# Moving the shift filter to channel-major tiles and the layer-norm scaling to ScalarE in a convolution and feed-forward kernel

## The chip, the cores and the metric

The kernel runs on one core of a Trainium2 chip. A time is the device time of one execution in microseconds (us). Kernels were timed in rounds together with the kernel before on the same chip. One core has five instruction streams that matter here, each working through its own list in order: TensorE (PE, matrix multiplication), VectorE (DVE, elementwise), ScalarE (ACT, elementwise with functions, here also the reader of most of PE's results), GpSimd (POOL) and SyncE (SP, which here only starts DMA transfers). The order inside each stream is settled when the kernel is built.

## The reference, cut to what matters

```python
def _layernorm(x): ...                       # (x - mean) / sqrt(var + 1e-5), no weights
# S = 2048 rows, D = 640 channels, F = 1728
k_shift[s] = sum_t k[s - t] * shift_k[:, t]  # 4 taps: the shift filter
kv = k_shift * v
y  = causal_convolution(kv, ssm_k)           # 2048 taps per channel, by FFT in the reference
y  = y + kv * ssm_D
h  = x + layernorm(x) * y                    # x is A_q
h2 = h + (silu(layernorm(h) @ w_gate) * (layernorm(h) @ w_up)) @ w_down
```

All tensors are bfloat16. One remark on correctness: at these input sizes the convolution branch is so small beside `x` that the plain comparison with the reference can't see an error in it. The kernels whose values matter here were therefore also compared in values with `k`, `v` and `shift_k` enlarged 16 times and `ssm_k` 512 times; all had a relative error of 0.0085.

## The kernel before: the parts that matter

The sequence is cut into four blocks of 512 rows. The convolution is done block by block with a 1024-point spectral transform as matmuls: `X[j]` is the spectrum of block j of `kv`, `H[p]` the spectra of the long filter, and `pair(j, p)` adds a complex product of 128x2560 tiles to `A[j + p]` on VectorE. Since the transform uses even and odd parts about the block's middle, a `fold` adds and subtracts the mirrored half first.

The shift filter has rows on partitions. Four shifted copies of each row are loaded, multiplied by weights spread over all partitions (`w4`), added and multiplied by `v`; the mirrored half comes from a TensorE matmul with a reversal matrix and a ScalarE copy:

```python
    def front_half(t, v):                                  # VectorE, 128x1280 each
        ks = [t[:, :, s, :] for s in range(4)]
        for s in (3, 2, 1, 0):
            nc.vector.tensor_mul(ks[s], ks[s], w4[:, 3 - s:4 - s, :].to_broadcast([P, 2, D]))
        nc.vector.tensor_add(ks[3], ks[3], ks[2])          # ... two more adds, then * v
    def fold(ta, tb):
        kv, kvr = tb[:, :, 3, :], ta[:, :, 2, :]
        nc.vector.tensor_add(xe, kv, kvr)
        nc.vector.tensor_sub(xo, kv, kvr)
```

The layer norm takes sums on ScalarE (`stats`), the power -1/2 on POOL and the scaling on VectorE. The scaled rows go through a DMA transpose to become the moving side of the feed-forward's first matmuls (the weights are the stationary side):

```python
    def ln_rstd(mv, n, tag):
        # ... va = variance + eps, two small VectorE operations
        nc.gpsimd.tensor_tensor(rs[:], va[:], mhalf[:, 0:n, :], op=ALU.pow)
    def ln_apply(out_, in_, mv, rs):
        nc.vector.tensor_scalar(out_, in_, mv, rs, op0=ALU.subtract, op1=ALU.mult)
    def to_ffn(m, mv, rs, x, hT):
        # ... for each of two row groups:
            ln_apply(hl[:], x[:, q, :], mv[:, s, 0:1], rs[:, s, :])
            nc.sync.dma_start_transpose(hT[:, :, q * P:(q + 1) * P], hl[:])
```

In the feed-forward each of 14 chunks takes ten 128x512 matmuls into a PSUM tile `pf`, of which there are two. ScalarE must read both halves of it (an eviction) before TensorE may use that buffer again:

```python
                nc.scalar.activation(sg[:z, :], pg[:z, :], ACT.Silu)
                nc.scalar.copy(uc[:z, :], pu[:z, :])
                nc.vector.tensor_mul(tT[:z, c * MB:(c + 1) * MB], sg[:z, :], uc[:z, :])
```

The main loop interleaves the convolution of block j + 1 with the feed-forward of block j by priorities.

## Time and profile before

The median is 327.9 us (327.0 to 329.5, four runs). Milestones from the TensorE timeline, in us from the span's start:

| | feed-forward 0 up / down starts | 1 | 2 | 3 | last matmul |
|---|---|---|---|---|---|
| before | 80.0 / 124.5 | 141.1 / 180.2 | 213.6 / 252.2 | 274.9 / 307.0 | 323.1 |

First the page's busy line of the kernel before: for each engine its busy us, the share of the span and the instructions. Over the whole span TensorE is the busiest.

```profile
PE 280.5 (86%) x1580; PEld 153.7 (47%) x1580; DVE 239.2 (73%) x334; ACT 171.4 (52%) x334; POOL 37.6 (11%) x33
```

An average over stages with different limits hides the bound. The next view is the table of stretches of the kernel before. Its columns are the stretch, its length, the busy us (and instructions) of each engine, the granted TensorE clock, the DMA share and the GB/s.

```profile
77.30:257.60 180.30, 162.59 (x886) 84.32 (x883) 172.36 (x224) 100.67 (x199) 22.43 (x11) 0.97 0.51 145
257.60:274.90 17.30, 14.41 (x101) 9.22 (x102) 11.37 (x25) 7.33 (x17) 3.51 (x4) 1.00 0.30 72
274.90:327.20 52.30, 48.23 (x252) 24.33 (x252) 9.24 (x18) 15.01 (x28) 2.00 (x2) 0.96 0.27 74
```

In the middle stretch, up to the end of the last spectral product, VectorE idles only 180.3 - 172.4 = 7.9 us. After it comes a tail of 69.6 us, which holds 14.41 + 48.23 = 62.6 us of TensorE work. The chain that ended last agrees that VectorE paces most of it (shares of the span by engine):

```profile
DVE 49%; PE 29%; DMA 6%; ACT 6%; issue 5%; POOL 4%; SPq 0%; DVEq 0%; POOLq 0%; ACTq 0%
```

The timeline of the kernel before, VectorE's last product and TensorE's longest gaps of the middle and end. Columns are start, length, engine, line, operation, output and inputs with count, and in brackets the idle time just before and what ended it.

```profile
204.81 0.72 PE L131 MATMUL ps<-xln,IJ 128*128 128x320 bf16 x4 [2.92 <-DVE hl L280]
212.05 1.25 PE L131 MATMUL ps<-k,IJ 128*128 128x320 bf16 x4 [6.52 <-DVE k L178]
...
256.12 1.49 DVE L251 TENSOR_TENSOR A_1383<-A_1383,T 128x2560 bf16<-128x2560 bf16 x1
...
274.89 1.39 PE L370 MATMUL pf<-hT,wg 128*128 128x512 bf16 x3 [2.82 <-DMA hT<-hl]
```

Two lines of the groups of instructions show what the change takes from VectorE: the filter's multiplications, and one of the groups of scalings (columns: line, engine, operation, names, shapes, count, then busy us and mean ns of one, then idle before).

```profile
L170 DVE TENSOR_TENSOR k<-k,w_91 128x1280 bf16<-128x1280 bf16 x24 | 19.1, 818 | 4.9 <-DMA k<-in_A_k_dram 4.9
...
L280 DVE TENSOR_SCALAR xln<-x,mv_826,rs_842 128x640 bf16<-128x640 bf16 x4 | 1.7, 444 | 0.9 <-POOL rs_842 L276 0.9
```

### The profile page before, as it was taken

Reading aid. Unit: us, or ns where it says so; the run is one execution under the profiler, and the core shown is the slowest. Engines: PE = TensorE matmul, PEld = TensorE weight load, DVE = VectorE, ACT = ScalarE, POOL = GpSimd, SP = SyncE. Lnnn points to the kernel's source line nnn. Section 1 sums busy time; section 2 is a strip of 40 time slices with the busy share of each in tenths; the row PEclk is TensorE's granted clock in tenths of the full one; section 3 lists DMA queues with packets and bytes.
Section 4 is the critical chain, followed back from the end, with each engine's and each line's share of the span. In section 5 each row is a group of like instructions: output and inputs, shape, how many; then the busy total and the mean of one; then the engine's idle time right before and its main releaser. Section 6 shows DMA issues by size and latency. Waiting matters only on the chain.

```text
span 327.2 us, 4271 instructions
## 1 busy us (share of the span) xinstructions
PE 280.5 (86%) x1580; PEld 153.7 (47%) x1580; DVE 239.2 (73%) x334; ACT 171.4 (52%) x334; POOL 37.6 (11%) x33
## 2 busy tenths in 40 slices
PE   2396888689699899989999896199999996999995
PEld 0254466456354356644445564034454662444563
DVE  0693398965999899899998999999969972122122
ACT  3138784897875438039748206964475080544300
POOL 6000001010000302510001071200010120000020
PEclk9999599999999999999999999679999998999999
DMA  7999900059687424536686503525525114355011
GB/s 231 373 311 224 331 0 3 21 119 376 198 296 211 116 79 124 101 98 166 167 216 227 173 20 95 123 73 144 155 58 141 41 40 100 99 151 132 2 40 41
DMA packets 67440, 45.94 MB, mean 140 GB/s; under 512 B 25614, under 2 KB 64846, under 8 KB 67420
## 3 DMA queue, kind: packets, MB, share of 16 engines
q1 hardware_dynamic: 66876, 44.29, 48.2%
q0 software_dynamic: 544, 1.39, 1.2%
q8 instruction: 12, 0.20, 0.2%
q14 instruction: 8, 0.07, 0.1%
HBM read 38.46 MB, written 2.62 MB: 126 GB/s over the span
## 4 chain that ended last, share of the span: by engine, by line
DVE 49%; PE 29%; DMA 6%; ACT 6%; issue 5%; POOL 4%; SPq 0%; DVEq 0%; POOLq 0%; ACTq 0%
PE pf L390 8%; PE pf L370 7%; PE pf L372 6%; DVE tT L379 4%; PE pf L214 4%; DVE k L170 3%; DVE T L250 3%; DMA hT<-hl 3%; DVE T L243 3%; PE ps L224 3%; DVE y L322 2%; DVE o L395 2%; DVE T L241 2%; DMA A_101<-in_A_k_dram 2%; DMA k<-in_A_k_dram 2%
## 5 line engine op out<-in xcount | busy, mean ns | idle before, releaser
L370 PE MATMUL pf<-hT,wg 128*128 128x512 bf16 (+1 forms) x280 | 72.2, 388 | 5.2 <-DMA hT<-hl 3.1
L372 PE MATMUL pf<-hT,wu 128*128 128x512 bf16 (+1 forms) x280 | 72.4, 385 | 0.0
L390 PE MATMUL pf<-wd,tT 128*128 128x320 bf16 x448 | 65.1, 299 | 0.0
L376 ACT ACTIVATE sg<-pf 128x512 bf16<-128x512 f32 (+1 forms) x56 | 33.4, 596 | 53.4 <-PE pf L372 52.4
L390 PEld LDWEIGHTS <-tT 128*128 128x128 bf16 x448 | 41.3, 97 | 23.1 <-issue 8.4
L379 DVE TENSOR_TENSOR tT<-sg,uc 128x512 bf16<-128x512 bf16 (+1 forms) x56 | 23.5, 419 | 32.0 <-ACT uc L378 31.9
L370 PEld LDWEIGHTS <-wg 128*128 128x128 bf16 (+1 forms) x280 | 27.4, 100 | 40.0 <-issue 7.5
L372 PEld LDWEIGHTS <-wu 128*128 128x128 bf16 (+1 forms) x280 | 28.1, 100 | 33.0 <-issue 2.8
L214 PE MATMUL pf<-wd,tT 128*128 128x320 bf16 x192 | 30.5, 317 | 8.7 <-POOL wd L448 3.8
L214 PEld LDWEIGHTS <-tT 128*128 128x128 bf16 x256 | 26.0, 102 | 21.7 <-issue 10.6
L378 ACT CAST uc<-pf 128x512 bf16<-128x512 f32 (+1 forms) x56 | 32.5, 581 | 0.0
L268 ACT ACTIVATE junk<-x 128x640 bf16<-128x640 bf16 x32 | 23.7, 741 | 9.5 <-DVE x L324 8.4
L400 POOL DMA_INDIRECT out_dram<-o,idx x8 | 15.7, 1968 | 88.2 <-DVE o L395 80.1
L269 ACT ACTIVATE junk<-x 128x640 bf16<-128x640 bf16 x32 | 23.7, 740 | 0.9
L170 DVE TENSOR_TENSOR k<-k,w_91 128x1280 bf16<-128x1280 bf16 x24 | 19.1, 818 | 4.9 <-DMA k<-in_A_k_dram 4.9
L395 DVE TENSOR_TENSOR o<-pf,x 128x640 bf16<-128x640 f32 x16 | 13.1, 818 | 12.1 <-PE pf L390 12.1
L224 PEld LDWEIGHTS <-WX 128*128 128x128 bf16 x128 | 13.2, 105 | 17.6 <-issue 7.1
L307 ACT COPY es<-ps 128x640 f32<-128x640 f32 x8 | 5.5, 693 | 27.7 <-PE ps L304 27.7
L224 PE MATMUL ps<-k,WX 128*128 128x320 bf16 x96 | 15.4, 298 | 2.4 <-DVE k L185 2.2
L322 DVE TENSOR_TENSOR y<-es,ps 128x640 bf16<-128x640 f32 x16 | 12.5, 813 | 0.7 <-PE ps L314 0.7
L132 ACT CAST x<-ps 128x640 bf16<-128x640 f32 x8 | 5.1, 691 | 14.8 <-DVE o L395 14.8
L216 ACT CAST G_95<-pf 128x640 bf16<-128x640 f32 x8 | 5.6, 696 | 13.7 <-PE pf L214 13.7
(175 smaller groups left out, 337.0 us busy)
## 6 DMA issues: line engine op xcount, KB each, us to landing
k<-in_A_k_dram SPq DMA_DIRECT2D x6, 1280.0 KB, 6.1
wg<-in_B_w_gate_dram SPq DMA_DIRECT2D x24, 320.0 KB, 3.2
wu<-in_B_w_up_dram SPq DMA_DIRECT2D x24, 320.0 KB, 3.8
wd<-in_B_w_down_dram SPq DMA_DIRECT2D x1, 2080.0 KB
v<-in_A_v_dram SPq DMA_DIRECT2D x5, 320.0 KB, 3.4
A_102<-in_A_k_dram SPq DMA_DIRECT2D x1, 1280.0 KB, 11.3
x<-in_A_q_dram SPq DMA_DIRECT2D x4, 320.0 KB, 5.3
xln<-in_A_q_dram SPq DMA_DIRECT2D x4, 320.0 KB, 3.2
```

The costliest lines, as they stand in the source:

```text
L170: nc.vector.tensor_mul(ks[s], ks[s], w4[:, 3 - s:4 - s, :].to_broadcast([P, 2, D]))
L214: nc.tensor.matmul(ps[:, h, 0:NH], WG[:, kt, ct * P:(ct + 1) * P], gT[p][:, kt, h * NH:(h + 1) * NH], start=(kt == 0), stop=(kt == 3))
L224: nc.tensor.matmul(ps[:, h, 0:NH], WX[:, kt, ct * P:(ct + 1) * P], src[:, kt, h * NH:(h + 1) * NH], start=(kt == 0), stop=(kt == 1))
L268: nc.scalar.activation(junk[:], src, ACT.Copy, scale=1.0 / D, accum_out=mv[:, 0:1])
L269: nc.scalar.activation(junk[:], src, ACT.Square, scale=D ** -0.5, accum_out=mv[:, 1:2])
L370: nc.tensor.matmul(pg[:z, :], wg[:, kt, cc * P:cc * P + z], hT[:, kt, :], start=(kt == 0), stop=(kt == 4))
L372: nc.tensor.matmul(pu[:z, :], wu[:, kt, cc * P:cc * P + z], hT[:, kt, :], start=(kt == 0), stop=(kt == 4))
L376: nc.scalar.activation(sg[:z, :], pg[:z, :], ACT.Silu)
L378: nc.scalar.copy(uc[:z, :], pu[:z, :])
L379: nc.vector.tensor_mul(tT[:z, c * MB:(c + 1) * MB], sg[:z, :], uc[:z, :])
L390: nc.tensor.matmul(ps[:, h, 0:NH], tT[:z, c * MB + m * P:c * MB + (m + 1) * P], wd[:z, c, h * NH:(h + 1) * NH], start=(c == 0), stop=(c == ...
L395: nc.vector.tensor_add(r3(o[:]), ps[:, :, 0:NH], r3(x[:, m, :]))
```

## The change

The intent: take work off VectorE, the bound of the middle stretch, and give it to ScalarE, which is half idle, and to DMA. For blocks 1 to 3, (1) `k` and `v` are loaded by DMA transposes, so that channels lie on partitions and a tap is a multiplication by one number per partition; (2) taps 1 and 3 run on ScalarE; (3) the mirror is a reversed operand of the fold; (4) the folded tile goes back to rows on partitions by five DMA transposes; (5) both layer-norm scalings run on ScalarE, which needs the shift -mean/std as an extra small POOL operation; (6) a block's filter and `pair(0, 3)` are issued earlier than before. Block 1's filter, on the other hand, is held back until the last sums and scalings of block 0 are in the list (`issue_after`). The diff's core:

```diff
+    def front_cm(kT, vT, xeo):
+        def tap(dst, s):
+            for c in range(5):
+                src = kT[:, c, 16 - s:16 - s + MB]
+                w = wT[:, c, s:s + 1]
+                if s in (1, 3):
+                    nc.scalar.activation(dst[:, c, :], src, ACT.Copy, scale=w)
+                else:
+                    nc.vector.tensor_scalar(dst[:, c, :], src, w, None, op0=ALU.mult)
         ... taps, three adds and the product with vT: 128x2560 each
+        lo, hi = p1[:, :, 255::-1], p1[:, :, 256:512]
+        nc.vector.tensor_add(vT[:, :, 0:256], hi, lo)
+        nc.vector.tensor_sub(vT[:, :, 256:512], hi, lo)
+        for c in range(5):
+            nc.sync.dma_start_transpose(xeo[:, :, c * P:(c + 1) * P], vT[:, c, :])
     ...
+    def ln_shift(mv, rs, n, tag):
+        nc.gpsimd.tensor_tensor(nm[:], mv[:, :, 0:1], rs[:], op=ALU.mult)
+    def ln_apply_act(out_, in_, nm, rs):
+        nc.scalar.activation(out_, in_, ACT.Identity, bias=nm, scale=rs)
     ... x_norm and to_ffn of blocks 1 to 3 call these two
     ... in the main loop:
-                xeo[n] = conv_front(n, z - 5000, z)
-            if n == 2:
-                A[3] = sp("A1")
-                pair(0, 3)
+                xeo[n] = conv_front(n, z - 9500, z - 7500)
     ...
             if n == 1:
                 A[2] = sp("G1")
                 pair(0, 2)
+                A[3] = sp("A1")
+                pair(0, 3)
+                prio(z + 3500)
                 pair(1, 1)
```

More of the change, by code (lines that the diff above doesn't have):

```diff
@@ L145 @@
     WI = cpool.tile([P, 8, 256], BF16, name="WI")
-    w4 = cpool.tile([P, 4, D], BF16, name="w4")
+    wT = cpool.tile([P, 5, 4], FP32, name="wT")
+    wTb = cpool.tile([P, 5, 4], BF16, name="wTb")
     Drow = cpool.tile([1, D], BF16, name="Drow")
@@ L155 @@
     T = spec.tile([P, 4, D], BF16, name="T")
+    w4 = T
     H, X, A = [G[0], None, G[2], G[3]], {}, {}
@@ L187, in fold, with load_front @@
         return xe, xo
-    def load_front(j, half):
-        t = front.tile([P, 2, 4, D], BF16, name="k", bufs=2)
-        load_k(nc.sync, t[:], j, half)
-        v = front.tile([P, 2, D], BF16, name="v")
-        load2(nc.sync, v[:], vv, j, half)
-        return t, v
-    def conv_front(j, p_load, p_calc):
-        ts = []
-        for half in (0, 1):
-            prio(p_load + 20 * half)
-            t, v = load_front(j, half)
-            prio(p_calc + 50 * half)
-            for _ in front_half(t, v[:]):
-                pass
-            if half == 0:
-                mirror(t[:, :, 3, :], t[:, :, 2, :])
-            ts.append(t)
-        return fold(*ts)
+    def load_front(j):
+        kT = front.tile([P, 5, MB + 16], BF16, name="kT")
+        nc.sync.dma_start_transpose(kT[:], kk[j * MB - 16:(j + 1) * MB, :])
+        vT = front.tile([P, 5, MB], BF16, name="vT")
+        nc.sync.dma_start_transpose(vT[:], vv[j * MB:(j + 1) * MB, :])
+        return kT, vT
@@ new lines, in front_cm @@
+    def front_cm(kT, vT, xeo):
[7 more added lines that the diff above has]
+                    nc.vector.tensor_scalar(dst[:, c, :], src, w, None, op0=ALU.mult)
+        pt = lambda: front.tile([P, 5, MB], BF16, name="pt", bufs=2)
+        p3, p2 = pt(), pt()
+        tap(p3, 3)
+        tap(p2, 2)
+        yield
+        nc.vector.tensor_add(p2[:], p2[:], p3[:])
+        yield
+        p1 = pt()
+        tap(p1, 1)
+        p0 = kT[:, :, 16:16 + MB]
+        tap(p0, 0)
+        yield
+        nc.vector.tensor_add(p1[:], p1[:], p0)
+        yield
+        nc.vector.tensor_add(p1[:], p1[:], p2[:])
+        yield
+        nc.vector.tensor_mul(p1[:], p1[:], vT[:])
+        yield
+        lo, hi = p1[:, :, 255::-1], p1[:, :, 256:512]
+        nc.vector.tensor_add(vT[:, :, 0:256], hi, lo)
+        yield
+        nc.vector.tensor_sub(vT[:, :, 256:512], hi, lo)
+        for c in range(5):
+            nc.sync.dma_start_transpose(xeo[:, :, c * P:(c + 1) * P], vT[:, c, :])
+        yield
@@ L209, in g_transform, with new_xeo @@
+    def new_xeo():
+        return front.tile([P, 4, D], BF16, name="xeo")
+    def conv_front(j, p_load, p_calc):
+        prio(p_load)
+        kT, vT = load_front(j)
+        prio(p_calc)
+        xeo = new_xeo()
+        for _ in front_cm(kT, vT, xeo):
+            pass
+        return xeo[:, 0:2, :], xeo[:, 2:4, :]
     def g_transform(p, cts=range(NCT)):
@@ L267, in stats @@
         junk = front.tile([P, D], BF16, name="junk")
-        nc.scalar.activation(junk[:], src, ACT.Copy, scale=1.0 / D, accum_out=mv[:, 0:1])
-        nc.scalar.activation(junk[:], src, ACT.Square, scale=D ** -0.5, accum_out=mv[:, 1:2])
+        nc.scalar.activation(junk[:], src, ACT.Copy, scale=-1.0 / D, accum_out=mv[:, 0:1])
+        return nc.scalar.activation(junk[:], src, ACT.Square, scale=D ** -0.5, accum_out=mv[:, 1:2])
     def ln_rstd(mv, n, tag):
@@ L279, in ln_apply @@
     def ln_apply(out_, in_, mv, rs):
-        nc.vector.tensor_scalar(out_, in_, mv, rs, op0=ALU.subtract, op1=ALU.mult)
+        return nc.vector.tensor_scalar(out_, in_, mv, rs, op0=ALU.add, op1=ALU.mult)
+    def ln_shift(mv, rs, n, tag):
+        nm = small.tile([P, n, 1], FP32, name="nm" + tag)
+        nc.gpsimd.tensor_tensor(nm[:], mv[:, :, 0:1], rs[:], op=ALU.mult)
+        return nm
+    def ln_apply_act(out_, in_, nm, rs):
+        nc.scalar.activation(out_, in_, ACT.Identity, bias=nm, scale=rs)
     def load_x(j, eng):
@@ L295, in x_norm @@
                 stats(x[:, q, :], mv[:, q, :])
+            rs = ln_rstd(mv[:], 4, "1")
+            nm = ln_shift(mv, rs, 4, "1")
+            for q in range(4):
+                ln_apply_act(xl[:, q, :], x[:, q, :], nm[:, q, :], rs[:, q, :])
+            return
         rs = ln_rstd(mv[:], 4, "1")
@@ L324, in add_row @@
         nc.vector.tensor_add(x[:, q, :], x[:, q, :], y[:])
-        stats(x[:, q, :], mv[:, s, :])
+        return stats(x[:, q, :], mv[:, s, :])
     def add_rows(m, es, po, x, xln):
@@ L332, in add_rows, with to_ffn @@
         return mv, ln_rstd(mv[:], 2, "2")
-    def to_ffn(m, mv, rs, x, hT):
+    def to_ffn(m, mv, rs, x, hT, on_act=True):
+        if on_act:
+            nm = ln_shift(mv, rs, 2, "2")
         for s in range(2):
@@ L337, in to_ffn @@
             hl = rot.tile([P, D], BF16, name="hl")
-            ln_apply(hl[:], x[:, q, :], mv[:, s, 0:1], rs[:, s, :])
+            if on_act:
+                ln_apply_act(hl[:], x[:, q, :], nm[:, s, :], rs[:, s, :])
+            else:
+                last = ln_apply(hl[:], x[:, q, :], mv[:, s, 0:1], rs[:, s, :])
             nc.sync.dma_start_transpose(hT[:, :, q * P:(q + 1) * P], hl[:])
+        return None if on_act else last
     def new_hT():
@@ L419 @@
     nc.gpsimd.dma_start(out=Drow[:], in_=A_ssm_D.partition_broadcast(1))
+    nc.gpsimd.dma_start(out=wTb[:], in_=A_shift_k.rearrange("(c p) j -> p c j", p=P))
+    nc.gpsimd.tensor_copy(wT[:], wTb[:])
     load2(nc.sync, v0[:, 0:2, :], vv, 0, 0)
@@ L470 @@
         po = inv_odd(A[0], 0)
-        t1, v1 = load_front(1, 0)
-        f1 = front_half(t1, v1[:])
+        k1, v1 = load_front(1)
         es1 = inv_even(A[0], 1)
-        drain(f1, 2)
         po1 = inv_odd(A[0], 1)
@@ L486 @@
         g_transform(2, range(3, 4))
-        add_row(1, 1, es1, po1, x0, xl0, mvb)
-        to_ffn(0, mva, rsa, x0, hT[0])
+        act0 = add_row(1, 1, es1, po1, x0, xl0, mvb)
+        to_ffn(0, mva, rsa, x0, hT[0], False)
         g_transform(2, range(4, 6))
-        drain(f1, 1)
         rsb = ln_rstd(mvb[:], 2, "2")
-        drain(f1, 1)
-        to_ffn(1, mvb, rsb, x0, hT[0])
+        dve0 = to_ffn(1, mvb, rsb, x0, hT[0], False)
         g_transform(2, range(6, 8))
-        t2 = front.tile([P, 2, 4, D], BF16, name="k", bufs=2)
-        load_k(nc.sync, t2[:], 1, 1)
-        v2 = sp("A1")[:, 0:2, :]
-        load2(nc.sync, v2, vv, 1, 1)
         wd = big.tile([P, NF, D], BF16, name="wd")
@@ L501 @@
         nc.sync.dma_start(out=wd[0:64, 13, :], in_=B_w_down[13 * P:FF, :])
-        g_transform(3, range(0, 4))
-        drain(f1)
-        mirror(t1[:, :, 3, :], t1[:, :, 2, :])
-        g_transform(3, range(4, 8))
+        g_transform(3)
     prio(3000)
-    drain(front_half(t2, v2))
-    xeo[1] = fold(t1, t2)
+    later = ExitStack()
+    later.enter_context(tc.issue_after(dve0.ins))
+    later.enter_context(tc.issue_after(act0.ins))
+    xeo1 = new_xeo()
+    drain(front_cm(k1, v1, xeo1))
+    xeo[1] = xeo1[:, 0:2, :], xeo1[:, 2:4, :]
     prio(3200)
@@ L535 @@
             x_norm(xin[n], xln[n])
+            later.close()
             hT[n] = inverse(A[n], xin[n], xln[n])
```

## The prediction

> **What bounds it now.** VectorE paces the middle: the stretch table shows DVE busy 172.4 of 180.3 us between 77.3 and 257.6 us, ScalarE 100.7; TensorE waits 11 us around 200 to 213 us. In the DVE timeline a 128x2560 bf16 product starts every 1.40 us, a 128x1280 one every 0.735. The Trainium skill, "VectorE: DVE Perf Modes", section "The perf-mode tier table", caps bf16 tensor_tensor at 2x and lets tensor_scalar reach 4x, which fits. After DVE's last spectral product (257.6 us) comes a tail of 69 us: inverse, layer norm, the end of feed-forward 2, feed-forward 3 (14 x 2.16 + 16.1 = 46.3 us, TensorE at its full pace).
>
> **What the change does.**
> - Filter on DVE, per block 1 to 3: was 18 x 0.735 = 13.2 us. Now 10 taps of 128x512 (estimate 0.27 us each, from 0.36 for 128x640 with two scalars), 4 x 1.40, 2 folds of 1280 with a reversed operand (0.735 if that keeps 2x, 1.4 if not): 9.8 to 11.1 us. Saves 2 to 3.4.
> - Layer-norm scaling of blocks 1 to 3 leaves DVE: 8 x 0.36 = 2.9 us per block. In all DVE saves about 16 us.
> - ScalarE gains 30 taps and 24 scalings, loses 6 mirror copies. The skill, "ScalarE: Activation LUTs", section "What ACT_TABLE_LOAD costs", adds about 93 ns per pointer operand; from the 0.64 us pace of the 128x640 passes I estimate 0.6 us a tap, 0.8 a scaling: busy 171 to about 205 us. Not a bound, but in order.
> - DMA: redundant row loads become transposes, and the folded result goes through five transposes per block (about 1.2 us of issue each, 2.6 to landing, read from those of hl): about 7 us between fold and transform that did not exist. Other pairs and the next filter fill it; for block 1 I expect 1 to 3 us of DVE idle.
> - The 4.9 us DVE wait for k at 72 us goes. In exchange hbuild and filter work that DVE did in gaps before 69 us now runs after block 0's norm, which should finish 1 to 2 us sooner.
>
> **Critical path.** Up to feed-forward 0's end (about 125 us before its down projection) I expect almost no gain. DVE then reaches its last spectral product at 236 to 240 us. The gain is not passed on whole: in the new order TensorE then still has 3.5 chunks of feed-forward 2 up, its down and feed-forward 3 to do, about 77 us instead of 69. That hides the last layer norm, so the wait of 2.8 us before feed-forward 3 goes. 238 + 77.4 + about 1.5 us gives 317.
>
> **Predicted: 317 us, 309 to 324 (8 in 10). Faster by over 2%: 0.75; within 2%: 0.22; slower: 0.03.**
>
> **What would show it.** DVE busy 239 to about 222 us; ACT about 205; taps near 0.35 us long, folds 0.82 (or 1.5); last spectral product at 236 to 240 us; no TensorE gap over 3 us between feed-forwards 2 and 3; the 11 us gap before feed-forward 2 shrunk to about 4; feed-forward 0's down projection starting where it did.
>
> **What would make it wrong.** Large transposes that land late or block the in-order SP queue, so weights come late; ScalarE stalling in order at a scaling that waits for POOL or an hl buffer, delaying the next SiLU; folds at 1x; or, the other way, TensorE ahead of DVE everywhere, when its own work (about 213 us after 79 us) would give 300.

## The result and the profile after

The change made the kernel slower: 338.8 us median (337.6 to 339.3, four runs) beside 327.9 us. The ratio is 1.032 (95% interval 1.027 to 1.037). A ratio here is the mean time of one kernel's fast runs over that of the other's in the same rounds, so it is not quite the ratio of the medians quoted.

| | feed-forward 0 up / down starts | 1 | 2 | 3 | last matmul |
|---|---|---|---|---|---|
| before | 80.0 / 124.5 | 141.1 / 180.2 | 213.6 / 252.2 | 274.9 / 307.0 | 323.1 |
| after | 76.6 / 123.5 | 143.9 / 199.8 | 221.6 / 270.2 | 286.6 / 317.0 | 333.2 |

The loss shows in two places: the up projection of feed-forward 1 took 55.9 us instead of 39.1, and that of feed-forward 2 took 48.6 us instead of 38.6. Not all of this is waiting: in the tables of stretches below each of the two holds 200 matmuls instead of 179 and 180, as a part of the next block's inverse moved into it (5.0 us of TensorE in each, beside 0 and 1.05 us before). What lies between gained: from down 1 to up 2 it is 21.8 us instead of 33.4, and from down 2 to up 3 it is 16.4 instead of 22.7. The page's busy line of the kernel after shows that the planned move did happen: VectorE lost 17.5 us and ScalarE gained 29.6.

```profile
PE 282.5 (84%) x1553; PEld 153.2 (45%) x1568; DVE 221.7 (66%) x304; ACT 201.0 (60%) x382; POOL 36.7 (11%) x44
```

The table of stretches of the kernel after, cut where feed-forward 0 starts, the last spectral product ends and feed-forward 3 starts. (The table of the kernel before starts 2.75 us ahead of its feed-forward 0, where VectorE's wait for `k` ends.)

```profile
76.60:253.80 177.20, 149.59 (x765) 75.32 (x774) 152.85 (x189) 119.74 (x231) 20.56 (x18) 0.95 0.46 114
253.80:286.60 32.80, 29.73 (x183) 17.10 (x182) 11.71 (x25) 15.08 (x32) 3.78 (x6) 1.00 0.35 92
286.60:336.90 50.30, 46.39 (x250) 23.91 (x252) 10.08 (x19) 15.02 (x28) 1.92 (x2) 1.00 0.28 79
```

Counted from the start of feed-forward 0 in both kernels (in the kernel before the stretch is then 177.55 us long, with VectorE busy 169.63), VectorE was busy 16.8 us less in the middle stretch, but the stretch shrank by only 0.4 us: VectorE's idle time went from 7.9 to 24.4 us. And more of TensorE's work was left for the tail: 29.73 + 46.39 = 76.1 us, 13.5 us more than before, so the tail grew from 69.6 to 83.1 us. The view of the chain that ended last doesn't help here. "Issue", time in which an engine waited for nothing that the profile shows, is now its largest part, and its longest pieces lie ahead of POOL instructions (33.3 us before the store at 130.18 us), where the view finds no releaser; it shows no cause:

```profile
issue 39%; PE 31%; ACT 12%; POOL 7%; DMA 5%; DVE 4%; SPq 2%; POOLq 0%; DVEq 0%; ACTq 0%
```

The waits view says more. First the one line of it from the kernel before (columns: engine, what waited, for what: us in total, times, longest us):

```profile
DVE tT L379 <- ACT uc L378: 31.9, 15, 7.1
```

Then the kernel after:

```profile
DVE tT L436 <- ACT uc L435: 56.1, 29, 8.2
...
PE pf L427 <- ACT uc L435: 11.0, 9, 2.6
...
PE ps L262 <- DMA xeo<-vT: 8.5, 5, 2.3
...
ACT hl L326 <- POOL nm_1579 L322: 7.8, 1, 7.8
```

VectorE waits for ScalarE's evictions, TensorE waits for the same evictions and for the new transposes, and ScalarE waits for POOL. The timeline around the start of feed-forward 1 shows these waits in place; which of them made the difference only the experiments can say. First POOL: a store of the block before stands ahead of the power of the norm; then comes the new shift.

```profile
130.18 1.15 POOL L457 DMA_INDIRECT out_dram<-o,idx  x1 [33.51 <-DVE va_894 L312]
131.37 0.97 POOL L314 TENSOR_TENSOR rs_897<-va_894,mhalf 128x2 f32<-128x2 f32 x1
132.41 0.20 POOL L322 TENSOR_TENSOR nm_899<-mv_879,rs_897 128x2 f32<-128x2 f32 x1
```

Then ScalarE, with its two pairs of scalings, the second of which waits 1.96 us more for POOL:

```profile
132.65 1.73 ACT L326 ACTIVATE hl<-x,nm_899,rs_897 128x640 bf16<-128x640 bf16 x2 [1.38 <-POOL nm_899 L322]
...
138.99 1.73 ACT L326 ACTIVATE hl<-x,nm_947,rs_945 128x640 bf16<-128x640 bf16 x2 [1.96 <-POOL nm_947 L322]
```

Then the queue of SyncE, where a line is a group of DMA issues with the time from the start of the first to the end of the last. The transposes of `hT` run to 142.46 us, and the five transposes to `xeo` stand behind them in the same queue. It looks as if the late scalings had pushed all this back; e1 below shows that they had not:

```profile
133.60 8.86 SPq L395 DMA_TRANSPOSE hT<-hl  x4
...
143.17 6.43 SPq L232 DMA_TRANSPOSE xeo<-vT  x5
```

And TensorE, which has the next block's transform in the middle of the up projection's list and so stops there:

```profile
143.86 0.58 PE L427 MATMUL pf<-hT,wg 128*128 128x512 bf16 x1 [3.57 <-DVE G_955 L289]
...
148.26 0.30 PE L262 MATMUL ps<-xeo,WX 128*128 128x320 bf16 x1 [0.98 <-DMA xeo<-vT]
150.78 2.02 PE L262 MATMUL ps<-xeo,WX 128*128 128x320 bf16 x7 [2.23 <-DMA xeo<-vT]
...
155.79 1.24 PE L427 MATMUL pf<-hT,wg 128*128 128x512 bf16 x5
...
167.38 2.24 PE L427 MATMUL pf<-hT,wg 128*128 128x512 bf16 x5 [2.40 <-ACT uc L435]
...
173.82 1.86 PE L427 MATMUL pf<-hT,wg 128*128 128x512 bf16 x5 [2.43 <-ACT uc L435]
```

While TensorE stands at `xeo`, no up projection comes out, so VectorE has its product of gate and up as the next instruction and nothing to put in (8.15 us of idle before 154.80 us). The 3.57 us before 143.86 us are put down to VectorE by the view, but the last transpose of `hT` lands at about that time too. The last two gaps are ScalarE's. Ahead of the first, its list held copies of the transform and sums of the norm until the eviction at 166.67 us; ahead of the second, before 173.21 us, it worked in order through the wait for POOL (2.12 us) and four scalings (3.35 us) that stand ahead of an eviction:

```profile
169.94 3.35 ACT L326 ACTIVATE xln<-x,nm_1484,rs_1482 128x640 bf16<-128x640 bf16 x4 [2.12 <-POOL nm_1484 L322]
173.21 0.56 ACT L435 CAST uc<-pf 128x512 bf16<-128x512 f32 x1
```

There is a second price of such gaps. In the list above five 128x512 matmuls take 1.24 us at 155.79 and 2.24 us after the gap at 167.38. The tables of stretches for the two up projections that lost show the granted clock (third number from the right). In the kernel before:

```profile
141.10:180.20 39.10, 36.78 (x179) 16.90 (x176) 37.90 (x52) 26.98 (x54) 1.04 (x1) 1.00 0.64 183
213.60:252.20 38.60, 38.11 (x180) 17.81 (x181) 35.45 (x45) 22.02 (x41) 1.57 (x1) 0.96 0.43 113
```

And in the kernel after. The clock is lower in the first, 0.88 instead of 1.00, but not in the second:

```profile
143.90:199.80 55.90, 46.59 (x200) 21.31 (x204) 44.46 (x56) 33.20 (x66) 2.70 (x2) 0.88 0.41 101
221.60:270.20 48.60, 40.57 (x200) 19.66 (x205) 35.45 (x47) 36.55 (x76) 2.72 (x5) 1.00 0.42 109
```

The Trainium skill, "TensorE: Matmul & The Clock Gate", section "Part 1: The HAM clock gate (the "warmup" mystery)", says that the array's clock is halved after an idle window and comes back after some microseconds of sustained work. This trace agrees in kind: the granted clock was 0.57 between 150 and 153 us and 0.64 between 168 and 172 us, both right after gaps. How much of the loss the clock made was not tested.

The same chain of POOL, scaling, transpose returns at the start of feed-forward 2, in POOL and ScalarE of the kernel after. Here the store took 3.57 us, and the power and the shift took longer as well:

```profile
210.34 3.57 POOL L457 DMA_INDIRECT out_dram<-o,idx  x1 [5.90 <-DVE va_1574 L312]
213.94 1.77 POOL L314 TENSOR_TENSOR rs_1577<-va_1574,mhalf 128x2 f32<-128x2 f32 x1
215.79 0.92 POOL L322 TENSOR_TENSOR nm_1579<-mv_1559,rs_1577 128x2 f32<-128x2 f32 x1
...
216.74 1.73 ACT L326 ACTIVATE hl<-x,nm_1579,rs_1577 128x640 bf16<-128x640 bf16 x2 [7.76 <-POOL nm_1579 L322]
```

All this is a reading of one trace, and it names at least four suspects: the scaling on ScalarE (with POOL's extra step), the taps on ScalarE, the five transposes to `xeo`, and the new order. The experiments separate them.

### The profile page after: what moved, and what is told of

The parts are those of the page before. It is cut to its first block, busy times and chain, and to the rows that moved or that the text cites. A ratio compares the mean times of both kernels' runs of the same rounds, so it can differ in the third digit from the quotient of the medians.

```text
span 336.9 us, 4280 instructions
## 1 busy us (share of the span) xinstructions
PE 282.5 (84%) x1553; PEld 153.2 (45%) x1568; DVE 221.7 (66%) x304; ACT 201.0 (60%) x382; POOL 36.7 (11%) x44
## 4 chain that ended last, share of the span: by engine, by line
issue 39%; PE 31%; ACT 12%; POOL 7%; DMA 5%; DVE 4%; SPq 2%; POOLq 0%; DVEq 0%; ACTq 0%
PE pf L447 8%; PE pf L429 7%; PE pf L427 7%; PE pf L252 5%; ACT junk L306 3%; ACT junk L307 2%; PE ps L262 2%; DMA A_102<-in_A_k_dram 2%; DMA out_dram<-o,idx 2%; POOL out_dram L457 1%; PE ps L365 1%; ACT A_2035 L264 1%; SPq L232 1%; DMA wu<-in_B_w_up_dram 1%; PE ps L355 1%
## 5 line engine op out<-in xcount | busy, mean ns | idle before, releaser
L429 PE MATMUL pf<-hT,wu 128*128 128x512 bf16 (+1 forms) x275 | 73.7, 393 | 0.2
L447 PE MATMUL pf<-wd,tT 128*128 128x320 bf16 (+1 forms) x448 | 64.7, 299 | 1.9 <-ACT uc L435 1.6
L447 PEld LDWEIGHTS <-tT 128*128 128x128 bf16 (+1 forms) x448 | 41.2, 97 | 25.6 <-issue 10.1
L252 PE MATMUL pf<-wd,tT 128*128 128x320 bf16 x192 | 29.6, 312 | 6.2 <-POOL wd L507 3.5
L252 PEld LDWEIGHTS <-tT 128*128 128x128 bf16 x256 | 25.7, 100 | 19.2 <-issue 8.5
L306 ACT ACTIVATE junk<-x 128x640 bf16<-128x640 bf16 x32 | 24.1, 754 | 4.0 <-DVE x L375 3.8
L262 PE MATMUL ps<-xeo,WX 128*128 128x320 bf16 x96 | 17.7, 321 | 9.3 <-DMA xeo<-vT 8.5
L262 PEld LDWEIGHTS <-WX 128*128 128x128 bf16 x128 | 13.5, 108 | 26.0 <-issue 12.5
L307 ACT ACTIVATE junk<-x 128x640 bf16<-128x640 bf16 x32 | 24.0, 750 | 0.4
L457 POOL DMA_INDIRECT out_dram<-o,idx x8 | 11.1, 1392 | 95.5 <-DVE o L452 52.3
L206 ACT ACTIVATE pt<-kT,wT 128x512 bf16<-128x512 bf16 x30 | 21.1, 758 | 0.6 <-DMA kT<-in_A_k_dram 0.6
L262 PE MATMUL ps<-A_103,WX 128*128 128x320 bf16 x32 | 7.2, 398 | 4.3 <-ACT x L132 4.1
## 6 DMA issues: line engine op xcount, KB each, us to landing
tT<-const_wg SPq DMA_DIRECT2D x2, 512.0 KB, 11.1
```

Of the source, the lines that this page charges most:

```text
L206: nc.scalar.activation(dst[:, c, :], src, ACT.Copy, scale=w)
L252: nc.tensor.matmul(ps[:, h, 0:NH], WG[:, kt, ct * P:(ct + 1) * P], gT[p][:, kt, h * NH:(h + 1) * NH], start=(kt == 0), stop=(kt == 3))
L262: nc.tensor.matmul(ps[:, h, 0:NH], WX[:, kt, ct * P:(ct + 1) * P], src[:, kt, h * NH:(h + 1) * NH], start=(kt == 0), stop=(kt == 1))
L306: nc.scalar.activation(junk[:], src, ACT.Copy, scale=-1.0 / D, accum_out=mv[:, 0:1])
L307: return nc.scalar.activation(junk[:], src, ACT.Square, scale=D ** -0.5, accum_out=mv[:, 1:2])
L429: nc.tensor.matmul(pu[:z, :], wu[:, kt, cc * P:cc * P + z], hT[:, kt, :], start=(kt == 0), stop=(kt == 4))
```

## The experiments

Theory A: the scaling on ScalarE is the main cost, since it makes the next block's input and the feed-forward's evictions wait for each other in one in-order list. Rival B: the five transposes between fold and transform. Rival C: ScalarE is simply too loaded, the taps included. Rival D: the new order of filters and pairs. The times are medians of four or five runs, all fast but for e13, where one of the five was slow and is left out. The order was changed back (e4) for blocks 2 and 3 only; block 1's later filter and the transposed loads were never tested alone.

| run | what it is | median us | ratio to before |
|---|---|---|---|
| after | the change | 338.8 | 1.032 |
| e1 | scaling back on VectorE | 326.5 | 0.997 |
| e2 | before, with only the scaling on ScalarE | 333.4 | 1.015 |
| e3 | taps back on VectorE | 334.7 | 1.021 |
| e4 | old order | 345.8 | 1.056 |
| e5 | scaling and taps on VectorE | 329.3 | 1.006 |
| e6 | power and shift on VectorE (wrong values) | 331.7 | 1.010 |
| e7 | e1 without the five transposes (wrong values) | 316.5 | 0.965 |
| e8 | only the second scaling back on VectorE | 332.9 | 1.017 |
| e9 | e1 with one transpose for five | 317.9 | 0.967 |
| e10 | e1 with TensorE transposes | 321.8 | 0.980 |
| e11 | after without the five transposes (wrong values) | 336.2 | 1.023 |
| e12 | e9 with another store order | 316.4 | 0.965 |
| e13 | after with another store order | 345.5 | 1.054 |
| e14 | after with one transpose for five | 329.0 | 1.003 |

### e1 to e4: one part at a time

e1, the layer-norm scaling of all blocks on VectorE again, and with it no shift step on POOL:

```diff
-            rs = ln_rstd(mv[:], 4, "1")
-            nm = ln_shift(mv, rs, 4, "1")
-            for q in range(4):
-                ln_apply_act(xl[:, q, :], x[:, q, :], nm[:, q, :], rs[:, q, :])
-            return
-    def to_ffn(m, mv, rs, x, hT, on_act=True):
+    def to_ffn(m, mv, rs, x, hT, on_act=False):
```

> The changed kernel with all layer-norm scaling back on DVE (24 scalings of about 0.36 us return, some 9 us of DVE), filter, taps and order kept. Theory A (ScalarE in order: scalings that wait for POOL and taps hold up the SiLU evictions, so TensorE waits in the up projections of blocks 1 and 2): 325 to 331 us, and the TensorE waits of 2 to 2.6 us for ScalarE near 166, 172 and 265 us go. Theory B (the five transposes between fold and transform, ahead of matmuls in TensorE's order, cost it): unchanged or worse, 338 to 344 us. Theory C (the new order of filters and pairs costs it): unchanged or worse too.

Measured: 326.5 us, ratio 0.997 (0.991 to 1.002). VectorE was busy 229.3 us, ScalarE 184.7. So giving VectorE 7.6 us of work back made the kernel 12 us faster. Theory A holds for most of the loss, but e1 is still no faster than the kernel before although VectorE is busy 10 us less.

The trace of e1 also corrects the reading above. Its feed-forward 1 starts no earlier than in the change (143.86 us there), after nearly the same wait, and its transposes to `xeo` start at 142.91 us, where the change has 143.17:

```profile
144.35 1.69 PE L422 MATMUL pf<-hT,wg 128*128 128x512 bf16 x4 [2.94 <-DMA hT<-hl]
```

So what the scaling cost came after this point: from the start of feed-forward 1 to that of 2 the change took 77.7 us and e1 68.6, and from there to feed-forward 3 65.0 and 60.7. Over the whole kernel, TensorE's waits for evictions came to 11.0 us in the change and 3.5 in e1.

e2, the counterpart: the kernel before, in which only the scaling of blocks 1 to 3 goes to ScalarE, with the shift on POOL:

```diff
+        nc.gpsimd.tensor_tensor(nm[:], mv[:, :, 0:1], rs[:], op=ALU.mult)
-            ln_apply(hl[:], x[:, q, :], mv[:, s, 0:1], rs[:, s, :])
+                ln_apply_act(hl[:], x[:, q, :], nm[:, s, :], rs[:, s, :])
... the same in x_norm
```

> The kernel before with only the layer-norm scaling of blocks 1 to 3 moved to ScalarE. Theory A: slower than before by 3 to 8 us (331 to 336), because the extra POOL step and the in-order ScalarE delay the feed-forward's input and its SiLU. Theories B and C: faster, 320 to 326 us, as DVE, which paces the middle, loses about 9 us of work.

Measured: 333.4 us, ratio 1.015 (1.011 to 1.020). The one part alone, on the old kernel, costs 5 us while it takes 8 us from VectorE's busy time (230.9 us). In its waits, ScalarE waits 8.6 us for POOL at the second scaling and 7.2 us at the first. The scaling is harmful by itself, not only in company of the rest.

e3, the taps of the change on VectorE again:

```diff
-                if s in (1, 3):
+                if s in ():
```

> The changed kernel with all four taps on DVE (15 more tensor_scalar of about 0.27 us, 4 us of DVE; ScalarE loses 30... no, 30 ScalarE taps of about 0.65 us in all three blocks, 20 us, go and 30 DVE taps of 0.27 us, 8 us, come). Theory A: 331 to 336 us. Theories B and C: unchanged to 5 us slower, 338 to 344.

Measured: 334.7 us, ratio 1.021 (1.017 to 1.026): 4 us faster than the change, and ScalarE is busy 183.8 us, about as little as in e1. So 17 us less on ScalarE helped a third as much as e1's 16 us less (both give VectorE about 8 us). ScalarE's load, rival C, is at most a small part of it; which instructions stand in its list, and for what they wait, counts more.

e4, the change with the old order of filters and pairs:

```diff
-                xeo[n] = conv_front(n, z - 9500, z - 7500)
+                xeo[n] = conv_front(n, z - 5000, z)
+            if n == 2:
+                A[3] = sp("A1")
+                pair(0, 3)
... and without pair(0, 3) and prio(z + 3500) at n == 1
```

> The changed kernel with the order of before for blocks 2 and 3: the filter at the priority of its own block, and the pair of block 0 with section 3 in its old place; scaling and taps stay on ScalarE. Theory C: 325 to 331 us. Theories A and B: 336 to 345 us, since the transposes and the ScalarE work stay, and the transposes are less hidden.

Measured: 345.8 us, ratio 1.056 (1.050 to 1.061). Rival D falls: within the change, the new order helps by 7 us.

### e5 to e8: which part of the scaling, and what else is lost

e5, scaling and taps both on VectorE (the edits of e1 and e3 together):

```diff
-                if s in (1, 3):
+                if s in ():
-    def to_ffn(m, mv, rs, x, hT, on_act=True):
+    def to_ffn(m, mv, rs, x, hT, on_act=False):
... and x_norm as in e1
```

> Changed kernel with both the scaling and all taps on DVE; what is left of the change are the transposed loads, the transposes of the folded result and the order. If ScalarE's time itself holds up the SiLU evictions (A1), this gains again over scaling-on-DVE alone (326.5): 320 to 325 us. If only the scalings' waits in ScalarE's order hurt (A2), the taps on ScalarE were free and 8 us more on DVE cost time: 327 to 333 us.

Measured: 329.3 us, ratio 1.006 (1.002 to 1.009), 3 us slower than e1. Once the scaling is off ScalarE, the taps are better there: they take 8 us from VectorE (237.2 in e5, 229.3 in e1). A tap has only one thing to wait for, an early load; in the change the taps waited 0.6 us in all. That the taps helped in e1 and hurt in the change (e3) says that the parts interact.

e6 takes POOL out of the chain: the power becomes a plain multiplication on VectorE, and the shift too is done there:

```diff
-        nc.gpsimd.tensor_tensor(rs[:], va[:], mhalf[:, 0:n, :], op=ALU.pow)
+        nc.vector.tensor_tensor(rs[:], va[:], mhalf[:, 0:n, :], op=ALU.mult)
-        nc.gpsimd.tensor_tensor(nm[:], mv[:, :, 0:1], rs[:], op=ALU.mult)
+        nc.vector.tensor_tensor(nm[:], mv[:, :, 0:1], rs[:], op=ALU.mult)
```

> Changed kernel, scaling still on ScalarE, but the two small POOL steps in its chain (the power -0.5 and the shift) are done as two tiny products on DVE, with wrong values on purpose[...]. Nothing in the chain to the scaling is behind POOL's stores any more. A2 (the waits in ScalarE's order, POOL's stores among them): most of the 12 us come back, 326 to 332 us. A1 (ScalarE's time): 336 to 339 us.

Measured: 331.7 us, ratio 1.010 (1.006 to 1.014). About 7 of the 12 us come back without POOL. That is the most that the way over POOL can have cost the scaling: e6 takes the power off POOL in every norm, and e1 still has it there, so a part of the 7 us may have nothing to do with the scaling (e1 with the power on VectorE was not run). About 5 us or more are left for the scaling's place on ScalarE; TensorE still waits 9.6 us for evictions (11.0 in the change).

e7 is e1 with the five transposes left out; the transform reads the folded tile as it lies, which gives wrong values:

```diff
-        for c in range(5):
-            nc.sync.dma_start_transpose(xeo[:, :, c * P:(c + 1) * P], vT[:, c, :])
... and the transform gets vT, seen as four tiles of 640 columns
```

> Scaling on DVE, and the five transposes after the fold taken away, wrong on purpose: the transform reads the folded tile as it lies, with the same shapes. Theory B as a second cost: 316 to 323 us against 326.5, and the TensorE waits for xeo near 148, 150, 223 and 225 us go. If the transposes were hidden: 325 to 328.

Measured: 316.5 us, ratio 0.965 (0.963 to 0.968), 10 us less than e1. This is what e1 still lacked. Rival B is right as well, for a second, separate cost.

e8 puts only the second scaling (`hl`) back on VectorE and leaves the first (`xln`) on ScalarE:

```diff
-    def to_ffn(m, mv, rs, x, hT, on_act=True):
+    def to_ffn(m, mv, rs, x, hT, on_act=False):
```

> Only the scaling before the feed-forward (hl, 12 instructions) back on DVE; the first layer norm's (xln, 12 instructions) stays on ScalarE. If the latency chain into the feed-forward is what hurt: about 328 us or less. If the xln scalings, which block the SiLU evictions in mid up projection, hurt as much: about 332. If those alone: 336 to 339.

Measured: 332.9 us, ratio 1.017 (1.014 to 1.020). Each scaling has about half of the 12 us: 6 us come back with `hl`, 6 us more with `xln`.

### e9 to e11: a cheaper way back to rows

In the change the five transposes take 6.43 us of SyncE's queue per block. e9 is e1 with a single transpose of all 20 blocks into a tile that is ordered by channel group; the transform's matmuls take 512 and 128 columns instead of twice 320:

```diff
-        for c in range(5):
-            nc.sync.dma_start_transpose(xeo[:, :, c * P:(c + 1) * P], vT[:, c, :])
+        nc.sync.dma_start_transpose(xeo.rearrange("p c k d -> p (c k) d"), vT[:].rearrange("p c l -> p (c l)"))
...
+                    for c0, c1 in ((0, 4), (4, 5)):
+                        nc.tensor.matmul(flat[:, c0 * P:c1 * P], WX[:, kt, ct * P:(ct + 1) * P],
+                                         src[:, c0:c1, kt, :], start=(kt == 0), stop=(kt == 1))
```

> Scaling on DVE as in e1, and the five transposes of a block's folded result made one transpose of 20 blocks, with the transform's matmuls split 512 + 128 columns over the new layout (right values). If the number of transposes (about 1.25 us of issue each) is what TensorE waits for: 320 to 324 us, between e1 (326.5) and e7 without transposes (316.5). If it is their volume or the landing: 325 to 328.

Measured: 317.9 us, ratio 0.967 (0.962 to 0.972), with right values, better than either expectation, and only 1.4 us above e7, which has no transposes at all. The issue of the second block's transposes on SyncE, in e1:

```profile
142.91 6.46 SPq L232 DMA_TRANSPOSE xeo<-vT  x5
```

and in e9:

```profile
140.05 2.62 SPq L231 DMA_TRANSPOSE xeo<-vT  x1
```

The tables of stretches of the two kernels, from the start of feed-forward 0 to the last spectral product and from there to the end. e1:

```profile
77.60:256.40 178.80, 160.10 (x832) 81.60 (x842) 161.43 (x215) 110.98 (x221) 14.53 (x11) 0.96 0.52 123
256.40:323.90 67.50, 62.71 (x362) 34.32 (x365) 20.78 (x42) 22.35 (x45) 5.41 (x6) 0.99 0.29 76
```

e9:

```profile
77.80:248.10 170.30, 157.33 (x832) 79.15 (x842) 160.96 (x215) 110.69 (x221) 14.40 (x11) 0.98 0.53 129
248.10:316.00 67.90, 62.71 (x362) 34.27 (x365) 20.84 (x42) 22.35 (x45) 5.42 (x6) 1.00 0.28 76
```

VectorE's work and the tail are the same in both. What differs is its idle time in the middle stretch: 17.4 us in e1, 9.3 us in e9. That is the cost of the five transposes, seen on the engine that paces the stretch. Compare also the tail: 67.9 us with 62.7 us of TensorE work, as in the kernel before, so TensorE has no more work left for the tail than there when the scaling is off ScalarE.

e10 does the way back with 20 TensorE transposes and two ScalarE copies per block instead of a DMA:

```diff
+                for c in range(5):
+                    nc.tensor.transpose(ps[:, k, c * P:(c + 1) * P], vT[:, c, l0:l0 + P], ident)
+            nc.scalar.copy(xeo[:, 2 * t:2 * t + 2, :], ps[:, :, 0:D])
```

> Scaling on DVE, and the folded result transposed on TensorE (20 transposes of 128x128 per block) with two ScalarE evictions per block, no DMA transposes after the fold (right values). TensorE gains about 2 us and ScalarE about 2.3 us per block. If the latency of the DMA path was the cost of 10 us: 318 to 322 us. If the ScalarE evictions in order cost as much: 325 to 328.

Measured: 321.8 us, ratio 0.980 (0.975 to 0.984): better than five DMA transposes by 5 us, worse than one by 4 us.

e11 asks whether the transposes cost as much in the change itself; it is the change with e7's edit:

```diff
-        for c in range(5):
-            nc.sync.dma_start_transpose(xeo[:, :, c * P:(c + 1) * P], vT[:, c, :])
```

> The changed kernel, scaling on ScalarE, with the transposes after the fold taken away (wrong on purpose). If the two costs add up (12 us for the scaling, 10 for the transposes): 327 to 331 us. If they are one and the same wait: 334 to 339, or else near 317.

Measured: 336.2 us, ratio 1.023 (1.018 to 1.028): only 2.5 us came back, not 10. In its waits ScalarE stands 16.4 us for POOL at `hl` and 11.7 us at `xln`, more than in the change, and POOL was busy 48.8 us instead of 36.7. This run alone would have said that the transposes hardly matter in the change, and that had to be tested with e14.

### e12 to e14: the best version, and the last questions

In the change's trace a POOL store stood ahead of the norm's power. e12 is e9 with the row groups of the down projection in the order 0, 1, 2, 3 for blocks 0 to 2, so that POOL's indirect stores (groups 2 and 3) come last:

```diff
-        for m in (2, 3, 0, 1):
+        for m in ((2, 3, 0, 1) if j == NB - 1 else (0, 1, 2, 3)):
```

> e9 (scaling on DVE, one transpose per block) with the down projections of blocks 0 to 2 in the row order 0, 1, 2, 3, so that POOL's indirect stores come after the powers of the next block's norm in POOL's order (right values). If the stores in front of a power still cost time there: 313 to 316 us. If not: 317 to 319.

Measured: 316.4 us (316.2 to 318.2), ratio 0.965 (0.962 to 0.969), right values. It is the fastest version with right values, 3.5% faster than the kernel before. It lies between the two expectations, and its interval overlaps that of e9, so the store order itself is not shown to help.

e13 is the same edit on the change:

```diff
-        for m in (2, 3, 0, 1):
+        for m in ((2, 3, 0, 1) if j == NB - 1 else (0, 1, 2, 3)):
```

> The changed kernel, scaling on ScalarE, with the same reordering of the stores and nothing else (right values). If POOL's stores in front of the power and the shift are most of what e6 gave back (7 of the 12 us): 331 to 334 us. If it was the two POOL steps themselves: 336 to 339.

Measured: 345.5 us (342.2 to 347.0, four fast runs; the fifth, 351.5 us, was slow), ratio 1.054 (1.049 to 1.059). Neither expectation came true. The profiled run was the fastest, at 342.2 us. What the edit aimed at did happen: ScalarE's waits for POOL at `hl` fell to 9.1 us, from 14.7 in the change. But other waits grew, and TensorE's waits for evictions went from 11.0 to 18.4 us. Two places of ScalarE's timeline, and TensorE's answer to the second, show how:

```profile
151.72 0.74 ACT L306 ACTIVATE junk<-x 128x640 bf16<-128x640 bf16 x1 [3.78 <-DMA x<-in_A_q_dram]
...
165.54 3.35 ACT L326 ACTIVATE xln<-x,nm,rs 128x640 bf16<-128x640 bf16 x4 [0.78 <-POOL nm L322]
168.80 0.58 ACT L433 ACTIVATE sg<-pf 128x512 bf16<-128x512 f32 x1
...
169.90 2.29 PE L427 MATMUL pf<-hT,wg 128*128 128x512 bf16 x5 [6.28 <-ACT uc L435]
```

The sums of block 2 waited for a load of `x` that SyncE issued at 147.80 us, behind the five transposes; and the transform's copies, the sums and the four scalings all stood ahead of the next SiLU, so TensorE stopped for 6.28 us. The order of ScalarE's list had shifted with the edit. That is read from one trace and not tested, and it is not an account of the whole 7 us.

e14 is the change, scaling on ScalarE included, with e9's single transpose:

```diff
-        for c in range(5):
-            nc.sync.dma_start_transpose(xeo[:, :, c * P:(c + 1) * P], vT[:, c, :])
+        nc.sync.dma_start_transpose(xeo.rearrange("p c k d -> p (c k) d"), vT[:].rearrange("p c l -> p (c l)"))
... and x_transform as in e9
```

> The changed kernel, scaling on ScalarE, with one transpose per block instead of five (right values): the fourth corner of scaling (ScalarE or DVE) by transposes (five or one). If the two costs are independent: 328 to 332 us, 9 below the changed kernel. If the waits of the scaling hide the transposes, as e11 suggests: 334 to 338.

Measured: 329.0 us, ratio 1.003 (0.999 to 1.008). This fills a square of two by two (medians in us):

| | five transposes | one transpose |
|---|---|---|
| scaling on ScalarE | 338.8 (the change) | 329.0 (e14) |
| scaling on VectorE | 326.5 (e1) | 317.9 (e9) |

The scaling costs 12.3 us with five transposes and 11.1 with one; the transposes cost 9.8 us with the scaling on ScalarE and 8.6 without. The two costs add to within about 1 us. e11's 2.5 us stays as an exception: when the transposes were left out altogether, the waits for POOL grew (above) and most of the gain was lost; whether that is the reason was not settled.

## Why the prediction was wrong

- **What bounds the kernel, and what the change does to busy times: right.** VectorE was to be busy about 222 us and was 221.7; ScalarE about 205 and was 201.0. The groups of instructions of the kernel after confirm the sizes: a VectorE tap near 0.35 us, and a fold with the reversed operand 0.82 us, so it kept the rate of the plain 128x1280 sum. In a row the taps came every 0.26 us (four in 1.14 us); by columns that is about the pace of a 128x2560 product (1.40 us), so a tap as a multiplication by one number per partition was not clearly cheaper per column.

```profile
L208 DVE TENSOR_SCALAR kT<-kT,wT 128x512 bf16<-128x512 bf16 x15 | 4.8, 350 | 0.0
...
L228 DVE TENSOR_TENSOR vT<-pt 128x1280 bf16<-128x1280 bf16 x3 | 2.5, 818 | 0.0
...
L206 ACT ACTIVATE pt<-kT,wT 128x512 bf16<-128x512 bf16 x30 | 21.1, 758 | 0.6 <-DMA kT<-in_A_k_dram 0.6
...
L326 ACT ACTIVATE xln<-x,nm_1484,rs_1482 128x640 bf16<-128x640 bf16 x4 | 3.4, 907 | 2.1 <-POOL nm_1484 L322 2.1
```

- **ScalarE's durations: right as paces.** The estimates of 0.6 us a tap and 0.8 a scaling were paces. Single records have 0.76 and 0.91 us, but they overlap in a row: three taps took 1.99 us and four scalings 3.35 us, which is 0.62 and 0.81 us for each one more. The Trainium skill, "ScalarE: Activation LUTs", section "What ACT_TABLE_LOAD costs", gives 186 ns plus 0.833 ns per column, and about 93 ns per pointer operand: an estimate from it is 0.71 us for a tap and 0.91 for a scaling, which the trace matches closely for the scaling, and with 7% more for the tap.
- **"Not a bound, but in order": right in words, not drawn into the sum.** The prediction costed ScalarE's new work by its busy time against an engine with room, and so at nothing. This is the first failing step. The experiments put 12 us on the scaling there (e1 against the change; e9 against e14 gives 11), of which at most about 7 come by the way over POOL (e6). The rest is left for the scaling's place in ScalarE's own order; no run isolates it. Its cost showed after the start of feed-forward 1, and TensorE's waits for evictions over the whole kernel were 11.0 us beside 3.5 in e1. The prediction did name this under what would make it wrong, "ScalarE stalling in order at a scaling that waits for POOL or an hl buffer, delaying the next SiLU", and gave it too little weight.
- **"Other pairs and the next filter fill it; for block 1 I expect 1 to 3 us of DVE idle": the second failing step.** The issue cost was right, 1.29 us each of 6.43 us. But for block 1 VectorE idled 4.2 us before 100.54 us, and for block 2 8.15 us, not all of it the transposes' doing (with scaling on VectorE the longest such wait was 5.46 us with five transposes, e1, and 2.24 us with one, e9). Pairs could not fill the time, because the next instruction in VectorE's list was a product that waited for an eviction, and the eviction for a matmul that stood behind TensorE's wait for the transposes. The five transposes cost 9 to 10 us in all (e1 against e7 and e9; the change against e14).
- **"DVE then reaches its last spectral product at 236 to 240 us": wrong, by the sum of the two.** It ended at 253.8 us. Of the 16.8 us that VectorE saved in the middle stretch, 16.4 were given back as idle time.
- **"About 77 us instead of 69" for the tail: the amount of work was right.** TensorE had 76.1 us of work left, about as reckoned, and the tail was 83.1 us long with its idle time. But it began 15 us later than planned.
- **Feed-forward 0 unchanged, no gap before feed-forward 3: right.** Its down projection started at 123.5 us instead of 124.5. The wait before feed-forward 3 is gone, and the wait right before feed-forward 2 is 1.55 us; but the time saved in those gaps was lost inside the up projections.
- **The new order: right to be neutral or good.** Within the change it is worth 7 us (e4, blocks 2 and 3).

That e7 and e9 come out at 316 to 318 us, where the prediction put the change, fits the diagnosis: with both neglected costs gone the kernel arrives near the predicted time. It is no proof of the sum, since e9's VectorE is busy 228.9 us and not 222.

What stays open: how far POOL's slower operations and the order of ScalarE's list each contribute when both move (e11 and e13 changed the list along with the wait that they aimed at), and why the taps on ScalarE hurt beside the scaling and help without it.

## What to carry to other kernels

Work moved off the busiest engine can cost more than its busy time, if it stands in the other engine's fixed order between two things that must alternate quickly: here a scaling that waits for POOL was put into the same list as the evictions that free TensorE's buffers, and it cost more than the VectorE time it saved. Before costing a new DMA step by its share of bandwidth, follow the chain through it: how long its issue holds the queue, what stands behind it in that queue, and which engine has its consumer next in line; here five small issues could be one large one. When busy times come out as planned and the time doesn't, compare the idle time of the pacing engine stretch by stretch, and undo the parts one by one: here one part cost 12 us, another 10, and two others were gains in the company in which they were tested.

## What the Trainium skill lacked or had wrong

- "DMA: Bandwidth & Descriptors" and "Advanced Engine Details and Errata" (section "X-Bar Transpose (TRN2)", which says that transposes are as fast as regular DMAs) give no measured time that the issue of a transpose holds its queue on this chip (the first has only the vendor's cycle counts for earlier generations). The runs show 1.19 to 1.29 us for a transpose of 128x512 or 128x640, 2.5 to 2.6 us for one of 128x2560 (two of the three in e9; the third took 4.19), and about 3.1 us for one of 512x640 from memory, where a plain load issue in the same queue took 0.37 to 0.53 us; landing took 2.4, 4.1 and 5.3 us. Five transposes held the queue 6.4 us, one of the same bytes 2.6 us.
- "Vector Engine (DVE) Microarchitecture Reference" lists an operand with a negative step as not measured; "VectorE: DVE Perf Modes" counts a step of minus one among those that qualify for the 2x mode, which agrees with the following. Here a sum of two 128x1280 bf16 tiles, one of them read backwards, took 0.818 us, the same as with both forward (0.820 us).
- "TensorE: Matmul & The Clock Gate" names an idle window of about 3.4 us as what lowers the clock. In the change a gap of 2.40 us, after a few shorter ones, was enough: five 128x512 matmuls took 2.24 us after it instead of 1.24 us. In the kernel before it was a gap of 2.82 us, with a granted clock of 0.52 in the 3.1 us after it. (The page also tells of frequent short idles that lower the clock, without their length.)
- None of the pages that I looked at gives the time of a tiny POOL operation between busy engines: here a power of 128x2 took 0.69 to 1.88 us and the multiplication after it 0.20 to 0.92 us, in one trace; the indirect stores took 0.96 to 3.57 us.
